# Cosine attention with a feed-forward layer on one core: the order and the size of the first loads

## The chip, the core and the metric

The kernel runs on one core of a Trainium2 chip. The metric is the device time of one launch in microseconds, the median over runs. The profile comes from one further execution, recorded by the hardware profiler.

## What is computed

Batch 8, 12 heads, 448 tokens, head size 64; then a feed-forward layer from 768 to 2048 and back over the 3584 tokens. Inputs and output are float32.

```python
q_n = q / (norm(q, axis=-1) + 1e-6)
k_n = k / (norm(k, axis=-1) + 1e-6)
scores = q_n @ k_n.T / tau                  # tau = 0.1
attn = softmax(scores)                      # over the keys
x = (attn @ v).transpose(0, 2, 1, 3).reshape(B * S, H * D)
h = x @ w_in
out = maximum(0.01 * h, h) @ w_out
```

## The kernel before

**Tiling.** The unit of work on q and k is a pair of heads, a slot `s`; six slots make one batch, and two slots make a quad `j`, for which values are loaded and multiplied together. The 448 tokens of a head are 384 (the main part, 128 partitions with three tokens each) and 64 (the remainder). A pair's tile holds q's three main columns, then a column with q's remainder in partitions 0 to 63 and k's in 64 to 127, then k's three main columns. So q's squares (`squares`, first of the two) read both remainders.

**Steps of a slot.** `squares` squares q and k, on POOL from slot 2 on; for slots 0 and 1 ScalarE and VectorE do it (L523 to L534). `sums` reduces them on VectorE (L195), in two parts. `roots` takes the norms on ScalarE (L202 to L205). `normalise` scales on VectorE (L215, L219) and writes `qn`. `transposes` turns `qn` around on PE (L233) and copies it from PSUM on VectorE (L257); slot 0 has its own copies, half on ScalarE, half on VectorE (L548). `scores` multiplies on PE (L276) and takes exps on ScalarE (L288). `totals` and `products` multiply the exps by ones and by the values on PE (L316), and `scale` writes `xT` on VectorE (L351).

**Order.** The schedule is written out by hand: every engine takes its instructions in the order of the program, and semaphores make it wait for data. The first batch has a prologue of its own, a loop over its six slots (`for s in range(NPAIR)`). In it VectorE takes `sums(n, (1,))` of the slot after next ahead of the qkT copy of the next slot. PE begins with 22 products of constants (`fill(WARM)`, L504). Behind the loop come the third quad's attention, the first feed-forward product of the first block (L374, with `w_in`), and then for each block its second product (L453, L411, with `w_out`) interleaved with the next batch's scores.

**Loads.** q and k come on SP's queue; in the beginning k's first parts are on ScalarE's. `load_first` loads main part (part 0) or remainder (part 1) of `n` slots of the first batch, `load_qk` one slot later on (four DMAs: L144, L145 and twice L147). Values and weights come on POOL's queue and are cast to bf16 on the way: `load_v(j)` a quad's values (L162), `load_v_rem` a batch's remainders (L169), `load_w_in(i)` a quarter of `w_in` (L106; quarters 0 and 1 are the first 1024 columns), `load_w_out` (L113) a half. `hold(x)` is a one-column copy on POOL, which keeps what POOL does next behind the tile `x`.

Of the kernel before, what the change touches and what calls it, by code (L numbers as in the profile page):

```python
# [16 lines left out]
def kernel(  # L17
# [10 lines left out]
    nc = tc.nc  # L28
# [75 lines left out]
    def load_w_in(i):  # L104
        n0, e = i // 2 * (D_ff // 2), i % 2
        gp.dma_start(  # L106
            out=w_in_sb[:, e::2, n0 : n0 + D_ff // 2], in_=w_in_r[e, :, :, n0 : n0 + D_ff // 2]
        )
# [9 lines left out]
    def main(x, b, h0, nh):  # L118
        return x[b, h0 : h0 + nh, 0:MAIN].rearrange("h (p t) d -> p h t d", t=3)
# [4 lines left out]
    def load_first(eng, x, part, s0, n):  # L124

        h0, i = 2 * s0, 0 if x is q else 1
        if part == 0:
            dst = raw0[:, s0 : s0 + n, :, 4 * i : 4 * i + 3]
            eng.dma_start(
                out=dst.rearrange("p s h t d -> p (s h) t d"), in_=main(x, 0, h0, 2 * n)  # L130
            )
        else:
            dst = raw0[64 * i : 64 * i + 64, s0 : s0 + n, :, 3]
            eng.dma_start(
                out=dst.rearrange("p s h d -> p (s h) d"),
                in_=x[0, h0 : h0 + 2 * n, MAIN:S].rearrange("h p d -> p h d"),
            )

    def load_qk(s):
        if s >= NSLOT:  # L140
            return
        b, h0 = s // NPAIR, 2 * (s % NPAIR)
        both = ldp.tile([128, 2, 7, D], F32, name="qk")
        nc.sync.dma_start(out=both[:, :, 0:3], in_=main(q, b, h0, 2))  # L144
        nc.sync.dma_start(out=both[:, :, 4:7], in_=main(k, b, h0, 2))  # L145
        for i, x in enumerate((q, k)):
            nc.sync.dma_start(  # L147
                out=both[64 * i : 64 * i + 64, :, 3],
                in_=x[b, h0 : h0 + 2, MAIN:S].rearrange("h p d -> p h d"),
            )  # L150
        raw[s] = (both[:, :, 0:4], both[:, :, 4:7])
# [5 lines left out]
    def load_v(j):  # L157
        if j >= B * NQ:
            return
        b, jj = divmod(j, NQ)  # L160
        vb[j] = vbp.tile([128, 4, 3, D], BF16, name="v_b")
        gp.dma_start(out=vb[j], in_=main(v, b, 4 * jj, 4))  # L162

    def load_v_rem(b, parts=slice(0, 4)):
        if b >= B:
            return
        x = vrb[b % 2].rearrange("p j g d -> p (j g) d")
        for lo, h0, h1 in ((0, 0, 2), (64, 2, 6), (0, 6, 10), (64, 10, 12))[parts]:
            gp.dma_start(  # L169
                out=x[lo : lo + 64, h0:h1], in_=v[b, h0:h1, MAIN:S].rearrange("h p d -> p h d")  # L170
            )
# [3 lines left out]
    def squares(s, engs=(gp, gp)):  # L175
        if s >= NSLOT:
            return
        tiles = []
        for x, eng, name in zip(raw[s], engs, ("sq0", "sq1")):
            sq = sqp.tile(list(x.shape), F32, name=name)  # L180
            if eng is nc.scalar:
                nc.scalar.activation(sq, x, func=AF.Square)
            else:
                eng.tensor_tensor(sq, x, x, op=ALU.mult)  # L184
            tiles.append(sq)
        sqs[s] = tiles

    def sums(s, parts=(0, 1)):
        if s >= NSLOT:
            return  # L190
        if s not in ss:
            ss[s] = smp.tile([128, 14], F32, name="ss")
        for i in parts:
            o = ss[s][:, 0:8] if i == 0 else ss[s][:, 8:14]
            nc.vector.tensor_reduce(  # L195
                o.rearrange("p (h t) -> p h t", h=2), sqs[s][i], axis=AX.X, op=ALU.add
            )

    def roots(s):
        if s >= NSLOT:  # L200
            return
        nc.scalar.activation(ss[s], ss[s], func=AF.Ln, bias=tiny)  # L202
        nc.scalar.activation(ss[s], ss[s], func=AF.Exp, scale=0.5)  # L203
        if s < 2:
            nc.scalar.activation(ss[s], ss[s], func=AF.Identity, bias=eps)  # L205
# [3 lines left out]
    def normalise(s):  # L209
        if s >= NSLOT:  # L210
            return
        r = smp.tile([128, 14], F32, name="r")
        if s >= 2:
            nc.vector.tensor_scalar_add(ss[s], ss[s], 1e-6)  # L214
        nc.vector.reciprocal(r, ss[s])  # L215
        qn[s] = qnp.tile([128, 7, 2, D], BF16, name="qn")
        for x, lo, hi, r0 in ((raw[s][0], 0, 4, 0), (raw[s][1], 4, 7, 8)):
            nt = hi - lo
            nc.vector.tensor_tensor(  # L219
                qn[s][:, lo:hi],  # L220
                x.rearrange("p h t d -> p t h d"),
                r[:, r0 : r0 + 2 * nt].rearrange("p (h t) -> p t h", h=2)
                .unsqueeze(3).to_broadcast([128, nt, 2, D]),
                op=ALU.mult,
            )
# [35 lines left out]
    def scores(s, kis):  # L261
        key_tiles([(s, ki) for ki in kis])
# [72 lines left out]
    def products(j, e, po=None, begun=False):  # L335
        b, jj = divmod(j, NQ)
        if po is None:
            po = banks(1, (j, e))
        pos[j, e] = po
        vm = vb[j].rearrange("p h t (d e) -> p h t e d", e=2)  # L340
        vr = vrb[b % 2].rearrange("p j g (d e) -> p j g e d", e=2)
        strip_products(
            j, po, lambda g, ki: vm[:, g, ki, e], None if begun else lambda g: vr[:, jj, g, e]
        )
# [123 lines left out]
                store(osb[c, ts], c, chunk_cols(c)[0] + ts * 128, 0, D_model)  # L468
        given_back(("rows", c, two))

    load_first(nc.sync, q, 0, 0, 1)
    load_first(nc.scalar, k, 0, 0, 1)
    load_first(nc.sync, q, 1, 0, 2)
    load_first(nc.scalar, k, 1, 0, 2)
    load_first(nc.sync, q, 0, 1, 1)
    load_first(nc.scalar, k, 0, 1, 1)
    for s, n, r in ((2, 2, 4), (4, 2, 0)):
        for part, m in ((0, n), (1, r)):
            if m:
                for x in (q, k):  # L480
                    load_first(nc.sync, x, part, s, m)
    tiny = cpool.tile([128, 1], F32, name="tiny")
    nc.vector.memset(tiny, 1e-18)
    eps = cpool.tile([128, 1], F32, name="eps")
# [16 lines left out]
    def fill(count):  # L501
        wm = banks(1)
        for i in range(count):
            nc.tensor.matmul(  # L504
                out=wm, lhsT=warm[:, :128], rhs=warm, start=(i == 0), stop=(i == count - 1)
            )
# [4 lines left out]
    def hold(x):  # L511
        seen = smp.tile([128, 1], F32, name="seen")
        gp.tensor_copy(out=seen, in_=x)  # L513
# [21 lines left out]
    normalise(0)  # L535
    load_qk(6)
    hold(qn[0][:, 6, 0, 0:1])
    load_v(0)
    squares(2)
    load_w_in(0)  # L540
    dst = qtp.tile([128, 7, 128], BF16, name="qkT")
    qkT[0] = dst.rearrange("p t c -> p (t c)")
# [11 lines left out]
    for s in range(NPAIR):  # L554
        j = s // 2 - 1 if s >= 2 else None
        even = s % 2 == 0
        n = s + 2 if s + 2 < NPAIR else None
        if s != 3 and s != 5:
            scores(s, (0,))
        if s == 1:  # L560
            roots(2)
        if j is not None and not even:
            products(j, 1)
        scores(s, (1,))
        fill(2)
        if s and n:
            sums(n, (0,))
        if s < 5:
            normalise(s + 1)
            if s != 1 and s < 4:  # L570
                load_qk(s + 7 - (s > 1))
        if j is not None and not even:
            scale(j, 0)
        if s < 5:
            hold(qn[s + 1][:, 6, 0, 0:1])
            squares(s + 3)
        if s == 0:
            load_v_rem(0, slice(2, 4))
        if s < 3:
            load_w_in(s + 1)  # L580
        if s in (1, 3):
            load_v(s // 2 + 1)
        if s == 3:
            load_w_out(0)
        elif s == 4:
            load_w_out(1, 4)
        if n:
            sums(n, (1,))
        scores(s, (2,))
        if s == 5:  # L590

            scale(j, 1)
            for m in range(SOON):
                pms[0, m] = banks(1, (0, m, 0), 4 + m)
            first(0, 0, range(KT - 2))
        elif not even:
            fill(2)
        if not even:
            scores(s, (3,))
        if s < 5:  # L600
            transposes(s + 1)
        if s == 0:
            sums(2, (0,))
        if s == 5:
            first(0, 1, range(KT - 2))
            sums(6)
            sums(7)
        elif not even:
            fill(2)
        if n and s:  # L610
            roots(n)
        if j is not None and not even and s < 5:
            scale(j, 1)
        if j is not None and even:
            totals(j)
            scores(s + 1, (0,))
            products(j, 0)
# [95 lines left out]
    for b in range(B):  # L713
# [15 lines left out]
        s = ready  # L729
# [50 lines left out]
```

## Time and profile before

| | |
|---|---|
| median of 3 runs | 416.69 us (416.69 to 416.94) |
| profiled execution, its own time | 417.32 us |
| its span, first to last instruction | 415.5 us |
| mean granted TensorE clock | 0.996 |
| busy share of PE / ScalarE / VectorE / POOL | 97% / 63% / 47% / 34% |
| HBM read / written | 45.61 MB / 11.01 MB |

The span leaves out what lies around the first and last instruction, here 1.8 us. A PE that counts as busy is not at its peak, since products are pipelined. Idle time of the other engines costs nothing as long as PE does not wait for them. Times within the profile count from the start of the span.

### The profile page before, as it was taken

What the parts mean: (1) busy time and instruction counts of PE and PEld (TensorE: products, weight loads), DVE (VectorE), ACT (ScalarE), POOL (GpSimd) and SP (SyncE); (2) the same over time, 40 slices, a digit from 0 to 9 for tenths busy, and PEclk for the clock granted to TensorE, in tenths of its full rate; (3) what the DMA queues carried; (4) which work ended last, traced back from release to release, by engine and by line L of the source; (5) the groups of instructions that cost most, each with busy time, mean ns of one, the idle gap of its engine ahead of it and who ended that gap; (6) DMA issues with size and microseconds to landing.
All of it is one profiled execution on the core that took longest, in us unless ns stands there. A gap on an engine that the chain in (4) does not pass through costs nothing.

```text
span 415.5 us, 10098 instructions
## 1 busy us (share of the span) xinstructions
PE 402.6 (97%) x4099; PEld 213.6 (51%) x4099; DVE 193.6 (47%) x412; ACT 260.1 (63%) x448; POOL 139.6 (34%) x212
## 2 busy tenths in 40 slices
PE   7687999999999999999999999999999999999996
PEld 2233655544555555544555555544555565544564
DVE  4785856256352725257261645156362654040021
ACT  3785669745785569845775559855776559934300
POOL 2884458055140634054231533153232530000000
PEclk9899999999999999999999999999999999999999
DMA  8999999576485966576386875677387753210023
GB/s 197 248 223 204 213 214 176 160 114 143 97 196 120 124 145 129 128 115 138 92 194 124 114 172 96 134 113 151 91 182 152 106 93 59 65 40 2 0 76 77
DMA packets 104767, 54.21 MB, mean 130 GB/s; under 512 B 70672, under 2 KB 99728, under 8 KB 104720
## 3 DMA queue, kind: packets, MB, share of 16 engines
q1 hardware_dynamic: 78640, 41.21, 42.8%
q0 software_dynamic: 25104, 11.80, 22.7%
q8 instruction: 32, 0.52, 0.6%
q10 hardware_dynamic: 976, 0.56, 0.5%
q14 instruction: 15, 0.12, 0.1%
HBM read 45.61 MB, written 11.01 MB: 136 GB/s over the span
## 4 chain that ended last, share of the span: by engine, by line
PE 91%; DMA 5%; DVE 2%; ACT 1%; POOL 1%; issue 0%; POOLq 0%; ACTq 0%
PE ps L374 35%; PE ps L453 30%; PE ps L316 11%; PE ps L276 7%; PE ps L411 5%; DMA v_b<-in_v_dram 3%; DMA raw<-in_k_dram 1%; PE ps L303 1%; DVE qn L219 1%; POOL sq L184 0%; PE ps L233 0%; DVE ss L195 0%; ACT pe L288 0%; ACT ss L202 0%; POOL w_in_sb L106 0%; DVE r L215 0%
## 5 line engine op out<-in xcount | busy, mean ns | idle before, releaser
L374 PE MATMUL ps<-xT,w_in_sb 128*128 128x384 bf16 (+1 forms) x768 | 147.7, 353 | 0.0
L453 PE MATMUL ps<-w_out_sb,hT 64*128 64x384 bf16 x1536 | 142.7, 323 | 0.0
L288 ACT ACTIVATE pe<-ps 128x896 bf16<-128x896 f32 x144 | 123.3, 918 | 23.2 <-PE ps L276 21.4
L381 ACT ACTIVATE hT<-ps 128x384 bf16<-128x384 f32 (+1 forms) x128 | 67.8, 544 | 73.8 <-PE ps L374 73.0
L374 PEld LDWEIGHTS <-w_in_sb 128*128 128x128 bf16 x768 | 74.2, 98 | 71.3 <-issue 3.4
L453 PEld LDWEIGHTS <-hT 64*128 64x128 bf16 x1536 | 73.6, 94 | 54.9 <-issue 3.3
L184 POOL TENSOR_TENSOR sq<-qk 128x512 f32<-128x512 f32 x84 | 77.4, 942 | 5.9 <-DMA qk<-in_k_dram 3.1
L463 DVE COPY osb<-ps 128x384 f32<-128x384 f32 x48 | 24.5, 553 | 76.0 <-PE ps L453 42.8
L276 PE MATMUL ps<-qkT 64*128 64x448 bf16 (+1 forms) x384 | 54.3, 357 | 3.1 <-ACT pe L288 1.9
L195 DVE TENSOR_REDUCE ss<-sq 128x6 f32<-128x384 f32 (+1 forms) x95 | 54.3, 610 | 0.3 <-POOL sq L184 0.3
L513 POOL CAST seen<-qn 128x1 f32<-128x1 bf16 x48 | 9.0, 187 | 132.9 <-DVE qn L219 125.0
L219 DVE TENSOR_TENSOR qn<-qk,r 128x512 bf16<-128x512 f32 x84 | 50.7, 645 | 1.4
L214 DVE TENSOR_SCALAR ss<-ss 128x14 f32<-128x14 f32 x46 | 9.3, 202 | 68.3 <-ACT ss L203 68.2
L162 POOL DMA_DIRECT2D v_b<-in_v_dram x24 | 18.5, 774 | 65.8 <-PE ps L316 65.8
L351 DVE TENSOR_TENSOR xT<-ps,rb 128x448 bf16<-128x448 f32 x48 | 27.8, 620 | 25.2 <-ACT rb L330 21.8
L316 PE MATMUL ps<-pe,v_b 128*32 128x448 bf16 x576 | 31.9, 353 | 1.8 <-DMA v_b<-in_v_dram 1.8
L276 PEld LDWEIGHTS <-qkT 64*128 64x128 bf16 (+1 forms) x384 | 16.7, 97 | 23.7 <-issue 10.5
L329 ACT ACTIVATE rb<-ps 128x448 f32<-128x448 f32 x24 | 12.9, 539 | 23.8 <-PE ps L316 23.8
L316 PEld LDWEIGHTS <-v_b 128*32 128x32 bf16 x576 | 15.1, 97 | 13.9 <-DMA v_b<-in_v_dram 2.1
L417 DVE COPY osb<-ps 128x384 f32<-128x384 f32 (+1 forms) x9 | 4.6, 514 | 36.6 <-issue 22.6
L288 ACT ACTIVATE pr<-ps 128x896 bf16<-128x896 f32 x24 | 21.3, 921 | 0.3 <-PE ps L276 0.2
L411 PE MATMUL ps<-w_out_sb,hT 128*128 128x384 bf16 (+1 forms) x144 | 21.0, 308 | 0.0
(49 smaller groups left out, 199.2 us busy)
## 6 DMA issues: line engine op xcount, KB each, us to landing
qk<-in_q_dram SPq DMA_DIRECT2D x42, 192.0 KB, 3.2
qk<-in_k_dram SPq DMA_DIRECT2D x42, 192.0 KB, 3.1
out_dram<-osb SPq DMA_DIRECT2D x30, 192.0 KB, 2.8
v_b<-in_v_dram POOLq DMA_DIRECT2D x24, 192.0 KB, 4.4
out_dram<-osb SPq DMA_DIRECT2D x12, 384.0 KB, 2.7
w_in_sb<-in_moe_w_in_dram POOLq DMA_DIRECT2D x4, 768.0 KB, 12.1
w_out_sb<-in_moe_w_out_dram POOLq DMA_DIRECT2D x1, 1536.0 KB, 18.4
w_out_sb<-in_moe_w_out_dram POOLq DMA_DIRECT2D x4, 384.0 KB, 19.7
```

The source lines that it names most:

```text
L184: eng.tensor_tensor(sq, x, x, op=ALU.mult)
L195: nc.vector.tensor_reduce(o.rearrange("p (h t) -> p h t", h=2), sqs[s][i], axis=AX.X, op=ALU.add)
L219: nc.vector.tensor_tensor(qn[s][:, lo:hi], x.rearrange("p h t d -> p t h d"), r[:, r0 : r0 + 2 * nt].rearrange("p (h t) -> p t h", h=2) .u ...
L276: nc.tensor.matmul(out=out[:, a, :S], lhsT=x[rows, c0:c1], rhs=x[rows, 0:S], start=True, stop=True,)
L288: nc.scalar.activation(out=dst, in_=sc[:, :, :S], func=AF.Exp, scale=inv_tau)
L316: nc.tensor.matmul(out=x[32 * g : 32 * g + 32, :S], lhsT=weights(g, ki) if ki < 3 else rem(g), rhs=pe[s][:, ki, a, :] if ki < 3 else pr[j] ...
L351: nc.vector.tensor_tensor(xT[m][:, 2 * jj + e, half * S : (half + 1) * S], pos.pop((j, e))[:, :S], rbs[j], op=ALU.mult,)
L374: nc.tensor.matmul(out=pm[:, :n], lhsT=w_in_sb[:, kt, m * 128 : (m + 1) * 128], rhs=xT[c // 2][:, kt, c0 : c0 + n], start=(kt == 0), stop= ...
L381: nc.scalar.activation(out=hT[c][:, m, :n], in_=pms.pop((c, m))[:, :n], func=AF.Prelu, alpha=0.01)
L411: nc.tensor.matmul(out=po2[:, :n], lhsT=hT[c][:, m, ts * 128 : (ts + 1) * 128], rhs=w_out_sb[:, m, lo : lo + n], start=(m == 0), stop=(m = ...
L453: last[i] = nc.tensor.matmul(out=po2[:, i, :HALF], lhsT=hT[c][rows, m, ts * 128 : (ts + 1) * 128], rhs=w_out_sb[rows, m, half * HALF : (ha ...
L463: nc.vector.tensor_copy(out=osb[c, ts][:, half * HALF : (half + 1) * HALF], in_=po2[:, i, :HALF])
```

## The change

It concerns the loads of the first batch only, and adds or takes away no arithmetic. First, the first batch's loads: pair 0's and pair 1's remainders, fetched by one DMA each for q and k before, are fetched pair by pair, pair 0's on SP's and ScalarE's queues and pair 1's on SP's alone; pair 2 is fetched by itself, then the remainders of pairs 2 and 3, the main part of pair 3, and last pairs 4 and 5 together. SP issues 15 loads ahead of pair 6 instead of 9; ScalarE issues 3 in both. Second, on POOL `squares(2)` stands ahead of `load_v(0)`. Third, the values of quads 1 and 2 are issued one place ahead of the third and of the last quarter of `w_in`; before, they were issued behind the third quarter and one step of the loop behind the last.

```diff
-    load_first(nc.sync, q, 0, 0, 1)
-    load_first(nc.scalar, k, 0, 0, 1)
-    load_first(nc.sync, q, 1, 0, 2)
-    load_first(nc.scalar, k, 1, 0, 2)
+    for part in range(2):
+        load_first(nc.sync, q, part, 0, 1)
+        load_first(nc.scalar, k, part, 0, 1)
     load_first(nc.sync, q, 0, 1, 1)
     load_first(nc.scalar, k, 0, 1, 1)
-    for s, n, r in ((2, 2, 4), (4, 2, 0)):
-        for part, m in ((0, n), (1, r)):
-            if m:
-                for x in (q, k):
-                    load_first(nc.sync, x, part, s, m)
+    for part, s, n in ((1, 1, 1), (0, 2, 1), (1, 2, 2), (0, 3, 1), (0, 4, 2), (1, 4, 2)):
+        for x in (q, k):
+            load_first(nc.sync, x, part, s, n)
...
     normalise(0)
     load_qk(6)
     hold(qn[0][:, 6, 0, 0:1])
+    squares(2)
     load_v(0)
-    squares(2)
     load_w_in(0)
...
         if s == 0:
             load_v_rem(0, slice(2, 4))
+        if s in (1, 2):
+            load_v(s)
         if s < 3:
             load_w_in(s + 1)
-        if s in (1, 3):
-            load_v(s // 2 + 1)
         if s == 3:
             load_w_out(0)
```

## The prediction

> **What bounds the kernel now.** I read the page first: its chain is 91% PE and 5% DMA, and PE is busy for 97% of the span. So the question is where those few per cent lie. The chain in order of time answers it. From 43.01 us on it is PE without a break; ahead of that it runs through loads and VectorE:
>
> ```profile
> 1.30 5.80 DMA raw<-in_k_dram
> 7.19 0.32 ACT sq L526
> ...
> 9.05 1.16 DVE qn L219 x2
> ...
> 12.83 2.41 DVE qn L219 x2
> 15.24 0.46 DVE ss L195
> 15.71 0.61 DVE qkT L257
> ...
> 16.36 0.38 PE ps L276 x2
> ...
> 21.91 0.76 POOL w_in_sb L106
> 22.67 13.26 DMA v_b<-in_v_dram
> ...
> 35.98 1.70 PE ps L316 x32
> ```
>
> Each line is start, duration, what ran. Two loads stand in it, the first remainder of k and the values of the second quad, and one VectorE step (L219) that takes 2.41 us the second time and 1.16 the first. Whatever is gained ahead of 43 us reaches the end whole, because PE does the same work without a break afterwards. Next the timeline, for what each of these steps waits on:
>
> ```profile
> 1.52 7.67 PE L504 MATMUL ps<-warm 128*128 128x512 bf16 x22 [1.52 <-DVE warm L487]
> 9.80 0.81 PE L233 MATMUL ps<-id,qn 128*128 128x128 bf16 x7 [0.61 <-DVE qn L219]
> 12.56 2.27 POOL L184 TENSOR_TENSOR sq<-raw 128x512 f32<-128x512 f32 x2 [1.40 <-DMA raw<-in_q_dram]
> 15.72 1.82 POOL L184 TENSOR_TENSOR sq<-raw 128x512 f32<-128x512 f32 x2
> 35.98 0.75 PE L316 MATMUL ps<-pe,v_b 128*32 128x448 bf16 x12 [1.80 <-DMA v_b<-in_v_dram]
> ```
>
> The bracket is the idle time before the row and what ended it. POOL's squares of pair 2 wait for the remainders of pairs 2 to 5, then run beside the second L219; both are slow (2.27 us against 1.82, 2.41 against 1.16). PE waits 1.80 us for values at 34.18. Last, the table by stretches, for the clock (columns: stretch, busy us of PE, PEld, DVE, ACT, POOL, granted clock, DMA share, GB/s):
>
> ```profile
> 13.93:17.35 3.42, 1.73 (x13) 0.62 (x13) 3.42 (x6) 1.60 (x3) 3.42 (x5) 1.00 1.25 270
> 17.35:20.76 3.41, 3.13 (x17) 1.35 (x17) 2.26 (x7) 3.29 (x7) 3.02 (x6) 0.50 1.09 200
> ```
>
> After a stretch in which PE was half idle, it ran one of 3.41 us at half clock. The DMA share is over 1, so the loads are saturated there: a load put forward is paid for by the ones behind it.
>
> **Pair 0's remainders alone (two heads, 32 KB, not four, 64 KB).** The k remainder was issued at 1.30 and landed at 7.10. Its queue had landed k's main part at 4.31, so 64 KB took 2.79 us more and half of it about 1.4: 5.7 us. Bounds: 4.8 (q's remainder took 0.89 us behind its main part, half of that 0.44) and 7.1. Square, sums, roots and L219 then move up by some 1.4 us, but PE's 22 warm-up products end at 1.52 + 7.67 = 9.19, and the transposes stand behind them. They start at 9.19, not 9.80. The copy behind them on VectorE, the sums of pair 1 behind that copy, and the roots at 11.63 move by those **0.6 us** and no more. For this the remainder need only land by 6.5.
>
> **Pair 1's remainders now go through SP's queue,** fourth and fifth there. ScalarE's squares of pair 1 (L534) wait for them, and behind L534 stands the first qkT copy. Interpolating SP's landings by amount of data (q of pair 1 at 7.36, q of pairs 2 and 3 at 9.15), they land near 7.8; needed by 8.75 if 0.6 us is to be kept. Hidden, by about 1 us.
>
> **Pair 2 by itself.** Before, it is complete when the remainders of pairs 2 to 5 are, 4.87 + 7.6 = 12.4. Now ahead of it lie three pairs instead of four and four remainders instead of six, each remainder counted at half a main part's time (in the trace, packets of 256 B take 18 ns and of 768 B 36 ns). On SP's queue that is the time of 92 main packets per DMA engine, where 72 were done at 9.15 and 104 at 11.0: about 10.2. Bounds: 9.7 (all remainders hidden behind main parts of the other queue), and 16.8 in the slow rival below. POOL's squares then run 10.2 to 12.0. The second L219 begins at 12.83 - 0.6 = 12.23, has no POOL squares beside it, and takes 1.16 as its other cases do: it ends at 13.4, not 15.24. VectorE's sums, the copy, the scores and the exps follow (0.46, 0.61, 0.4): the exps of pair 1 start at 15.0 instead of 16.77. ScalarE is free by 14.4. The front gains **1.8 us**; bounds 0.6 (if L219 still meets the squares) and 2.4 (when ScalarE is free).
>
> **The clock.** PE's idle time between 11.2 and 16.4 shrinks by those 1.8 us, so it is about 66% busy in the stretch that was 51% busy. In the half-rate stretch two warm-ups took 1.04 us against 0.60, the remainder scores 0.59 against 0.38, the transposes 0.93 against 0.55. ScalarE idles only 0.58 us behind this, so at most 0.4 us come back. I take **0.2**, the middle, since only one such stretch is in the trace. The Trainium skill ("TensorE: Matmul & The Clock Gate", Part 1) says that half rate comes after at least one idle stretch of about 3.4 us; here it came after one that was 51% busy, so the trace differs, and by the page's wording the sum would have 0 in this place.
>
> **Values ahead of w_in's third and last quarter.** `load_v(1)` passes one POOL issue (0.78 us); `load_v(2)` passes one `hold`, one pair of squares and w_in's last issue. POOL idles 0.89 us ahead of the hold at 27.20, which covers the extra 0.81 us there. `squares(2)` passes `load_v(0)`, which then issues at 12 instead of 10.4 and lands near 19; first used at 24.94. The transfers go in order: w_in's quarters 2 and 3 land at 30.1 and 34.7, values 1 at 35.94, w_in's last at 39.6, values 2 at 40.68. With the third quarter behind it, values 1 lands at 35.94 - 4.58 = 31.4. PE asks at 34.18 - 2.0 = 32.2, so the **1.8 us** wait goes. Next in line is values 2: without w_in's last quarter (39.63 - 35.94 = 3.7) they land at 37.0. PE uses them at 41.14, so they allow 4.1 us in all, and no stall follows from a gain of 3.8. w_in's last quarter moves to 40.7; its columns start with the ninth block of first products, at about 50 - 4.
>
> **The six extra SP issues.** In the trace, from the fourteenth SP load on, each issue starts when the one eight before it has landed (15.32 behind 15.31, 17.00 behind 16.98). With fifteen loads before pair 6, not nine, pair 6 issues near 10 instead of 8.95 and lands by 18.5; POOL squares it at 27.4 - 2. Hidden, at nothing; uncovered it would cost that 1 us. Later, w_out's last part lands at 60.2, and the loads of pairs 10 to 13 will now start 4 us sooner beside it: it may reach 62, and is used from about 64.
>
> **Sum.** 1.8 + 0.2 + 1.8 = 3.8 us. The profiled execution took 417.32 us (span 415.5), so 413.5; it is 0.6 above the median of 416.69, so by the median **412.9**.
>
> **The rivals.**
> *Values only.* Pair 2 lands at 11.5 or later, L219 still runs beside POOL's squares, and only the transposes' 0.6 us stays of the front: 0.6 + 1.8 = 2.4, giving 414.3. For it: a load issued at 3.21 took 7.8 us, and the ninth SP issue will be near 5.5. Against: that load had 104 such packets ahead, all full.
> *No difference.* PE's wait hangs on the slowest DMA engine, not on the place in the queue: values 1 are nearly all through by 34, two microseconds before they land. If that engine keeps them until 35, and the front keeps nothing, 1 us at most is left: 416.2. Against: w_in ahead of them lands just 1.24 us earlier.
> *Slower: small transfers in series.* VectorE takes the sums of pair 2 ahead of pair 1's qkT copy, so pair 2's last remainder gates pair 1's scores. One SP issue in the trace took 1.88 us. If the fourth to ninth all do, the ninth goes out at 2.6 + 5 x 1.88 = 12.0; with the 4.8 us that a remainder of pair 7 (issued at 13.74) took to land, pair 2 is there at 16.8. Squares, sums, copy and the step to PE add 1.82 + 0.55 + 0.62 + 0.1: scores at 19.9 against 16.36, a loss of 3.5, less the 1.8 of the values: 1.7 slower, 418.4. It takes all the gain from a landing of 15.1 on, and is measurably slower from 16. Against: that 1.88 us issue was a load of twice the size with five large ones unfinished ahead of it.
> The Trainium skill ("DMA: Bandwidth & Descriptors", Rules for kernel authors) speaks for this rival: many small transfers should be joined, and under 64 KB mostly overhead is paid. Its fixed cost of about 2 us for each of the two more transfers ahead of pair 2, if paid in series, would put pair 2 at 14.2, and by that the kernel would gain about 1 us. Here 192 KB landed 3.2 us after issue and 64 KB 3.6, so a fixed part is there, but four transfers were under way at once.
>
> **How the numbers follow.** Forecast 0.66; values only 0.17; no difference 0.06; slower 0.11. A measurement can tell 0.2%, some 0.8 us, from no change. Faster is forecast and values only, 0.83; same 0.06; slower 0.11. The range reaches down to 411.8 (the front at 2.4, the clock at 0.4, values 1.8 and the 0.25 us by which runs of before differ, with values 2 some 0.7 us earlier than worked out) and up to 415.0 (values only, with half of the wait for values left); outside lie about 0.2.
>
> **What would show it.** Right: the row with in_k's remainder ends before 6.5; the seven transposes (L233) start at 9.2 straight behind the warm-ups; POOL's first squares start near 10.2 without the 1.40 us wait behind a load; the second L219 takes under 1.5 us for its two; no half clock near 17 to 21; the first `v_b` products have no wait for DMA, start near 32.2, and PE goes unbroken from about 39.2. Wrong: L534 or POOL's first squares waiting for a remainder past 11; PE waiting for `v_b` at either place; a wait for `w_in_sb` or `w_out_sb` behind 43 us, where there is none now.

## The result and the profile after

The kernel after takes 415.03 us, median of five runs (414.21 to 415.49); five runs of before on the same chip gave 416.69. The ratio is 0.9955, 95% interval 0.994 to 0.997: 1.66 us faster, less than half of the 3.8 us forecast. The profiled execution took 415.49 us, span 413.7, clock 0.996; against the 415.5 of before the span is 1.8 shorter.

First the end of the chain (start, duration, what ran), to be laid beside the chain of before. From 40.89 us on it is PE, and what PE waits for last are again values, now those of quad 2:

```profile
23.30 15.85 DMA v_b<-in_v_dram
39.19 1.70 PE ps L316 x28
40.89 3.68 PE ps L374 x22
```

Further back the chain runs through a load of pair 6, but that link is no wait. It hangs VectorE's L219 at 20.08 on a load that landed at 20.29, when L219 had begun; the timeline has L219 0.04 us behind the reciprocal of L215. Who ended a wait is inferred, so a link like this one is worth a look at the rows beside it. What did change is in SP's own timeline (start and duration of an issue):

```profile
4.62 0.47 SPq L129 DMA_DIRECT2D raw<-in_k_dram  x1
6.77 0.61 SPq L134 DMA_DIRECT2D raw<-in_q_dram  x1
```

The seventh load of SP went out at 4.62, the eighth at 6.77, straight behind the landing of q of pair 1, which was issued at 2.04 and landed at 6.75. SP's waits in the first 30 us name the same (us in total, times, longest):

```profile
SPq L134 <- DMA raw<-in_q_dram: 1.7, 1, 1.7
```

What the DMA engines did meanwhile, in the table by stretches (stretch, busy us of PE, PEld, DVE, ACT, POOL, granted clock, DMA share, GB/s). Before:

```profile
6.00:8.00 2.00, 2.00 (x8) 0.79 (x7) 0.29 (x1) 0.46 (x2) 0.00 (x0) 1.00 1.05 347
8.00:10.00 2.00, 1.39 (x10) 0.54 (x8) 1.19 (x3) 1.61 (x5) 1.60 (x3) 1.00 1.25 238
```

After:

```profile
6.00:8.00 2.00, 2.00 (x10) 0.71 (x8) 1.00 (x3) 1.75 (x5) 0.92 (x2) 1.00 0.74 210
8.00:10.00 2.00, 1.82 (x15) 0.72 (x14) 1.94 (x5) 0.69 (x3) 0.85 (x3) 1.00 0.56 90
```

The share falls from over 1 to 0.74 and 0.56, and the rate from 238 to 90 GB/s. By 11 us the DMA records of before add up to 2185 KB, those of after to 1750: 435 KB had not been fetched (a KB is 1024 bytes here). They are not made up later: by 31 us it is 6768 KB against 6288. The front itself came early, as the timeline of after shows (start, us, engine, line, operation, count; in brackets the idle time before and what ended it):

```profile
8.14 0.81 PE L233 MATMUL ps<-id,qn 128*128 128x128 bf16 x7
10.18 1.82 POOL L184 TENSOR_TENSOR sq<-raw 128x512 f32<-128x512 f32 x2 [1.32 <-DMA raw<-in_k_dram]
11.18 1.84 DVE L219 TENSOR_TENSOR qn<-raw,r 128x512 bf16<-128x512 f32 x2
14.54 0.92 ACT L288 ACTIVATE pe<-ps 128x896 bf16<-128x896 f32 x1 [1.26 <-PE ps L276]
...
32.59 0.75 PE L316 MATMUL ps<-pe,v_b 128*32 128x448 bf16 x12 [1.38 <-DMA v_b<-in_v_dram]
39.19 0.75 PE L316 MATMUL ps<-pe,v_b 128*32 128x448 bf16 x12 [1.07 <-DMA v_b<-in_v_dram]
73.76 0.55 PE L276 MATMUL ps<-qkT 64*128 64x448 bf16 x4 [0.46 <-DMA qkT<-qn]
```

The exps of pair 1 start at 14.54, against 16.77 before: 2.2 us. But PE waits for values twice, 1.38 + 1.07 us, where it waited 1.80 once, and at 73.76 there is a wait that before did not have. The first feed-forward products behind the third quad (L374) begin at 40.82 (before 42.95): 2.1 us there, 1.5 us behind the wait of 0.46 (the values' remainders, L303, at 77.57 against 79.07), 1.8 at the end of the span.

### The profile page after: what moved, and what is told of

The parts are those of the page before. It is cut to its first block, busy times and chain, and to the rows that moved or that the text cites. A ratio compares the mean times of both kernels' runs of the same rounds, so it can differ in the third digit from the quotient of the medians.

```text
span 413.7 us, 10099 instructions
## 1 busy us (share of the span) xinstructions
PE 400.9 (97%) x4088; PEld 213.6 (52%) x4099; DVE 193.2 (47%) x412; ACT 259.9 (63%) x448; POOL 139.4 (34%) x212
## 4 chain that ended last, share of the span: by engine, by line
PE 88%; DMA 8%; SPq 2%; POOL 0%; DVE 0%; issue 0%; POOLq 0%
PE ps L374 35%; PE ps L453 29%; PE ps L316 10%; PE ps L276 7%; PE ps L411 5%; DMA v_b<-in_v_dram 4%; DMA qk<-in_q_dram 2%; DMA qkT<-qn 1%; PE ps L303 1%; DMA raw<-in_q_dram 1%; SPq L134 1%; SPq L129 1%; POOL sq L184 0%; PE ps L233 0%; DVE qn L219 0%
## 5 line engine op out<-in xcount | busy, mean ns | idle before, releaser
L374 PE MATMUL ps<-xT,w_in_sb 128*128 128x384 bf16 (+1 forms) x760 | 147.3, 352 | 0.4
L374 PEld LDWEIGHTS <-w_in_sb 128*128 128x128 bf16 x768 | 74.1, 98 | 71.3 <-issue 3.4
L219 DVE TENSOR_TENSOR qn<-qk,r 128x512 bf16<-128x512 f32 x84 | 51.4, 653 | 2.0 <-DVE r L215 0.6
L214 DVE TENSOR_SCALAR ss<-ss 128x14 f32<-128x14 f32 x46 | 8.8, 190 | 67.6 <-ACT ss L203 67.6
```

The lines of the kernel that those rows point to most:

```text
L219: nc.vector.tensor_tensor(qn[s][:, lo:hi], x.rearrange("p h t d -> p t h d"), r[:, r0 : r0 + 2 * nt].rearrange("p (h t) -> p t h", h=2) .u ...
L374: nc.tensor.matmul(out=pm[:, :n], lhsT=w_in_sb[:, kt, m * 128 : (m + 1) * 128], rhs=xT[c // 2][:, kt, c0 : c0 + n], start=(kt == 0), stop= ...
```

## Experiments

**The theory, T.** The gain of the front is real, and it is spent on the values because the DMA engines run dry between 6 and 10 us. They run dry because SP stands until an earlier load has landed, while few bytes are under way and the next loads are small. The letters of the rivals are those of the expectations. The first four kernels were timed beside before at 416.64 us, the next four at 416.61.

**Values alone** (before, with only their order changed):

```diff
+        if s in (1, 2):
+            load_v(s)
         if s < 3:
             load_w_in(s + 1)
-        if s in (1, 3):
-            load_v(s // 2 + 1)
```

> The kernel before with the third part of the change alone: values of quads 1 and 2 one place ahead of w_in's third and last quarter; first loads and squares(2) as before. Theory T (the change saves PE's wait for values, but its small first loads leave the DMA idle: SP and ScalarE share eight completion semaphores, and SP stood from 5.09 to 6.77 us for the landing of q of pair 1; 435 KB fewer were moved by 11 us, some 2.1 us of DMA time, and that is missing when the values land): here the first loads are the old ones, so values 1 land near 31.4 and values 2 near 37.0, PE waits for neither, and the gain is the 1.8 us of the old wait: 414.9 us. Rival R1 (the place in POOL's queue counts for less than worked out, the slowest DMA engine sets the landing): values 2 land near 39, as in the changed kernel, and values 1 near 32.5; then the time is also about 414.9, but the landings tell the two apart.

Measured: 414.76 us, ratio 0.994 (0.9919 to 0.9962). The values of quads 1 and 2 land at 31.73 and 36.54, and in the timeline neither product has a bracket:

```profile
33.07 0.75 PE L316 MATMUL ps<-pe,v_b 128*32 128x448 bf16 x12
38.42 0.74 PE L316 MATMUL ps<-pe,v_b 128*32 128x448 bf16 x12
```

The third part of the change, by itself, gains 1.9 us: the 1.8 that the prediction gave it. It is as fast as the whole change.

**Loads alone** (after, with the values in their old places: the same edit taken back).

> The changed kernel with the values back in their old places (behind w_in's third quarter, and one step of the loop behind its last). Theory T: the front is some 2.2 to 2.9 us early as in the changed kernel, but the DMA is 2.1 us behind, so values 1 land near 38 instead of 35.9, PE waits about 6 to 7 us for them, and the kernel is slower than before by about 2 us: 418.7 us. Rival R1 (the small loads cost the DMA nothing, the places of the values were mis-sized): values 1 land at 35.9 as before and the time is that of before, 416.7 us, within 0.3.

Measured: 419.49 us, ratio 1.0055 (1.0036 to 1.0073): slower than before by 2.9 us. Only 1734 KB had come by 11 us. The values of quad 1 land at 36.06, where T said 38 and R1 35.9, so on this landing T was wrong and R1 right. They were issued earlier, though, at 21.40 against 22.67 in before, and took 14.66 us against 13.26. The loss showed in another way. PE came early and waited longer, and ran the next stretch at half clock, as timeline and table by stretches have it:

```profile
36.11 0.75 PE L316 MATMUL ps<-pe,v_b 128*32 128x448 bf16 x12 [3.19 <-DMA v_b<-in_v_dram]
36.96 1.35 PE L316 MATMUL ps<-pe,v_b 128*32 128x448 bf16 x12
```

```profile
33.37:36.78 3.41, 0.67 (x16) 0.43 (x20) 0.00 (x0) 1.27 (x2) 3.15 (x5) 1.00 1.22 230
36.78:40.20 3.42, 3.42 (x30) 0.87 (x22) 2.10 (x4) 0.92 (x1) 0.00 (x0) 0.50 1.25 203
```

PE was busy for 0.67 us of 3.41, then twelve products took 1.35 us and not 0.75. This execution took 418.66 us; ten runs lie between 417.16 and 420.10. The values of quad 2 land at 42.22, the values' remainders (L303) are multiplied at 80.74 (before 79.07).

**The same eighteen loads in another order** (after; pair 1's remainders go out ahead of q of pair 1, so the load whose landing SP waits for is a small and early one):

```diff
+    for x in (q, k):
+        load_first(nc.sync, x, 1, 1, 1)
     load_first(nc.sync, q, 0, 1, 1)
     load_first(nc.scalar, k, 0, 1, 1)
-    for part, s, n in ((1, 1, 1), (0, 2, 1), (1, 2, 2), (0, 3, 1), (0, 4, 2), (1, 4, 2)):
+    for part, s, n in ((0, 2, 1), (1, 2, 2), (0, 3, 1), (0, 4, 2), (1, 4, 2)):
```

> The changed kernel with the same 18 transfers of the same sizes on the same queues, but pair 1's two remainders are issued on SP ahead of q's main part of pair 1. By the rotation of the eight semaphores the loads from the seventh SP issue on then wait for small transfers that land at about 5, not for q of pair 1 (6.755 in the changed kernel). Theory T with the wait as its cause: SP's stand from 5.09 to 6.77 is gone, by 11 us 250 to 350 KB more have been moved than the changed kernel's 1750, values 2 land near 37.5 to 38, and the time is 413.3 to 414.0 us. Rival R2 (not the wait, but the 0.5 to 0.65 us that SP takes for each small issue starves the DMA): SP issues earlier, but bytes at 11 us rise by under 100 KB and the time stays at 414.7 to 415.0.

Measured: 413.01 us, ratio 0.9897 (0.9871 to 0.9923), an interval apart from that of after. In the timeline SP's eighth load (the first row) goes out at 5.30, not 6.77, behind the landing of pair 1's q remainder at 5.29, and the values are there when PE asks:

```profile
5.30 0.61 SPq L134 DMA_DIRECT2D raw<-in_q_dram  x1
...
31.55 0.75 PE L316 MATMUL ps<-pe,v_b 128*32 128x448 bf16 x12
36.98 0.75 PE L316 MATMUL ps<-pe,v_b 128*32 128x448 bf16 x12
```

And by stretches the DMA engines stay busy from 8 us on:

```profile
8.00:10.00 2.00, 1.84 (x15) 0.76 (x16) 1.89 (x5) 0.66 (x2) 0.18 (x1) 1.00 1.04 222
```

By 11 us 2175 KB had come, 425 more than after. The front is no faster than that of after (exps of pair 1 at 14.62), so the 2.0 us come from what is behind it: values 1 at 31.02 and 2 at 36.94 (after 32.55 and 39.15), and the products of L374 that follow begin at 38.61 (40.82). Neither the number nor the size of the transfers has changed, so these did not cost it, and R2 falls.

**Remainders of pairs 1 to 3 on POOL's queue** (after; SP is rid of four small loads):

```diff
-            load_first(nc.sync, x, part, s, n)
+            load_first(gp if part and s < 4 else nc.sync, x, part, s, n)
```

> The changed kernel with the four remainder loads of pairs 1, 2 and 3 issued from POOL, whose completion semaphores are its own, and which idles until 7 us; SP has 11 loads ahead of pair 6 instead of 15. Theory T: fewer loads pass through the eight semaphores and SP gets to the large ones sooner; bytes by 11 us come back to near the 2185 KB of before (over 2000), values 2 land near 37.2, PE's two waits for values are under 0.3 us in all, and the time is 412.8 to 413.5 us, unless remainders of pair 1 land later than 8 from this queue. Rival R2 expects nearly the same, since SP also issues fewer small loads; rival R1 (landings set by the slowest engine) expects 414.5 to 415.0, with values 2 still near 39.

Measured: 412.74 us, ratio 0.9893 (0.9872 to 0.9914). By stretches and in the timeline:

```profile
8.00:10.00 2.00, 1.92 (x16) 0.72 (x14) 2.00 (x5) 1.26 (x3) 2.00 (x5) 1.00 1.07 288
```

```profile
11.29 1.16 DVE L219 TENSOR_TENSOR qn<-raw,r 128x512 bf16<-128x512 f32 x2
13.97 0.92 ACT L288 ACTIVATE pe<-ps 128x896 bf16<-128x896 f32 x1 [0.58 <-PE ps L276]
...
70.72 0.55 PE L276 MATMUL ps<-qkT 64*128 64x448 bf16 x4 [0.50 <-DMA qkT<-qn]
```

The share is over 1, 2377 KB had come by 11 us, values 1 and 2 land at 29.29 and 36.07, and the products of L374 begin at 37.74. This is what the prediction had drawn for the change itself, with L219 at 1.16 us. SP stands here too: its seventh load goes out at 7.28, 2.0 us behind the end of the sixth issue, and this costs nothing. The wait of half a microsecond for pair 11's `qkT` is left.

**Six tiny loads** (values alone, plus six SP loads of 256 B each into a tile that nothing reads, at three places among the first loads; the large loads stay large):

```diff
+    def tiny_loads(i):
+        for n in (i, i + 1):
+            nc.sync.dma_start(out=scrap[:, n], in_=q[0, 0, n : n + 1])
```

> The kernel of the first experiment (old first loads, new order of the values) with six more SP loads of 256 bytes into a tile that nobody reads: two each behind q of pair 1, behind the main parts of pairs 2 and 3, and behind the remainders of pairs 2 to 5. So SP has 15 loads ahead of pair 6, as in the changed kernel, but every real load keeps its old size and order. Theory T (a load holds one of eight semaphores and half a microsecond of SP's time however small it is): fewer bytes are under way, SP stands for the landing of earlier loads, 200 to 450 KB less than the first experiment's 2238 are moved by 11 us, values 2 land 1 to 2.5 us later than its 36.5, and the time rises from 414.8 to 415.5 to 417. Rival R3 (what costs is the size of the split loads themselves, the overhead of small transfers within the DMA engines): 1.5 KB more do nothing, bytes at 11 us within 100 KB of 2238, time within 0.5 of 414.8.

Measured: 414.06 us, ratio 0.9932 (0.9917 to 0.9947). T expected a loss and there was none: it is no slower than values alone. SP did stand, as the timeline shows (these two tiny loads take 1.48 us with what is between them), and 227 KB less had come by 11 us:

```profile
5.32 1.48 SPq L475 DMA_DIRECT2D scrap<-in_q_dram  x2
```

But by stretches the engines were not dry behind it:

```profile
8.00:10.00 2.00, 1.40 (x11) 0.60 (x10) 2.00 (x5) 1.12 (x3) 1.30 (x3) 1.00 1.12 267
```

While SP stood, the main parts of pairs 2 and 3, two large transfers, were under way. The values land at 31.74 and 36.54, as without the tiny loads. So T has to be narrowed: more loads and a standing SP are not enough; few bytes must also be in flight. The traces of the five kernels let that be added up. At 8.0 us the loads of q, k and values that had been issued, less the bytes that had been moved, came to about 850 KB in before, 70 in after, 460 in the reordered kernel, 745 with the remainders on POOL and 490 here. By 31 us the last three had moved 6674, 6770 and 6652 KB, near the 6768 of before; after was at 6288.

**A later place for pairs 13 and 14** (the kernel with the remainders on POOL; their loads go one step later, behind the transposing DMAs of pairs 10 and 11, whose place in SP's queue is the disputed matter, theory D):

```diff
-        load_qk(s + 4)
+        for n in {9: (), 10: (13,), 11: (14, 15)}.get(s, (s + 4,)):
+            load_qk(n)
```

> The kernel with the remainders on POOL, and on SP's queue the loads of pair 13 and pair 14 each one step later, behind the transposes by DMA of pair 10 and pair 11. In that kernel, as in the changed one, PE waits 0.5 us at 70.7 for pair 11's transposed tile, which was issued at 64.6 and landed at 70.7, behind loads of pairs 13 and 14; before, it was issued at 69.1 and landed in 3.5 us. Theory D (the backlog of the DMA, met some 4 us sooner, now makes the transposes late): without those loads in front the tile lands by 69, the wait is gone, and the time is 412.2 to 412.4. Rival: the tile is late because of w_out and the values on POOL's queue, which share the DMA engines; then the wait stays and the time is 412.7.

Measured: 412.6 us, ratio 0.9897 (0.9883 to 0.9912). Pair 11's transposing DMA lands 3.7 us after its issue, and the products of 70.98 have no bracket:

```profile
65.77 1.26 SPq L251 DMA_TRANSPOSE qkT<-qn  x1
...
70.98 0.54 PE L276 MATMUL ps<-qkT 64*128 64x448 bf16 x4
```

The late wait is therefore one behind loads in the same queue. Its worth is not settled by the time. The same kernel without this edit was run again beside it:

> The kernel with the remainders of pairs 1 to 3 on POOL once more, beside the next two on the same chip: 412.7 us as before.

It gave 413.59 us, ratio 0.9914 (0.9895 to 0.9933), where it had given 412.74; the intervals of all three overlap, so between 0.1 and 1.0 us is all that can be said. Nor do the profiles settle it: in that of the later place PE waits 0.6 us for the values of quad 2, which it does not in the first profile of the kernel without the edit. The two profiles of one and the same kernel differ in the clock: one has no stretch at half rate behind 6 us, the other has one at 14.55.

**Values back in their old places, with the remainders on POOL:**

> The kernel with the remainders on POOL, with the values back in their old places. Theory T: with the DMA no longer starved the front is about 2.4 us early, PE asks for values 1 near 30.5, and they land where 4.6 us of w_in's third quarter put them, near 34; PE waits some 3.5 us, at most 1.5 to 2 us are gained, and if the wait is followed by a stretch at half clock as in the second experiment, nothing: 414.8 to 416.7 us. Rival R1 (the place of the values counts for little): 412.7 to 413.2.

Measured: 417.14 us, ratio 1.002 (0.9999 to 1.0041), somewhat above T's band and far from R1's. In the timeline PE waits for values twice:

```profile
34.51 0.75 PE L316 MATMUL ps<-pe,v_b 128*32 128x448 bf16 x12 [1.83 <-DMA v_b<-in_v_dram]
40.59 0.75 PE L316 MATMUL ps<-pe,v_b 128*32 128x448 bf16 x12 [0.56 <-DMA v_b<-in_v_dram]
```

Even with the DMA engines fed, an earlier front brings nothing without the values' new order. All of it together, each as the recorded ratio to before, which differs by up to 0.16% from the quotient of the medians:

| first loads | values in old places | values ahead of w_in |
|---|---|---|
| as before | 1 | 0.9940 |
| as in the change | 1.0055 | 0.9955 |
| the same loads, pair 1's remainders first | not run | 0.9897 |
| remainders of pairs 1 to 3 on POOL's queue | 1.0020 | 0.9893, again 0.9914 |

The last two rows of the right column beat both kernels, by 3.0 to 3.9 us against before; so does the kernel with pairs 13 and 14 put back, 4.0 us.

## Why the prediction was only partly right

**Where it held.** The direction and most landings did. The k remainder of pair 0 landed at 5.34 (worked out: 5.7), pair 1's last remainder at 7.35 (7.8), pair 2 was complete at 10.0 (10.2), POOL's first squares ran at 10.18, and PE's transposes followed straight behind the warm-ups, at 8.14 instead of 9.2, because the full clock was granted earlier in this execution (from 4.78 us, not 7.11). The earlier clock is luck, and so in part is the landing of pair 2. It was worked out from a queue in which packets follow each other without a gap, but its remainders were issued at 6.77 and 7.43, behind SP's stand, and the last of them landed at 10.0 from engines whose share was 0.56. The order of the values was worth what was said, shown by itself. The rule that under 64 KB mostly overhead is paid (the Trainium skill, "DMA: Bandwidth & Descriptors", Rules for kernel authors), which had spoken for the slower rival, does not decide here: the eighteen transfers of after and of its reordered twin are the same, and the twin is 2.0 us faster.

**The failed step** is "The six extra SP issues ... Hidden, at nothing". The prediction had seen that an issue waits for the landing of the load eight before it, but counted SP's loads alone, "from the fourteenth SP load on", and looked for the price at pair 6 (which went out at 11.63, not near 10). The trace of before showed it sooner: SP's sixth load went out at 3.99, behind the landing of its first at 3.97, and its seventh at 4.87, behind its second at 4.86. The issue records name the semaphores: the loads of SP and ScalarE take eight in turn (101, 102 and 104 to 109). In after SP's third load signals 104, and its eighth, the next to use 104, waits for it. With ScalarE's three counted in, that is eight loads apart in this turn, and in the reordered kernel the eighth issue again follows SP's third landing (5.30 behind 5.29). For 1.7 us SP could issue nothing, and what came next were two loads of 64 KB at 0.65 us an issue.

**What hung on it** is the sentence "The transfers go in order", with values 2 "at 37.0". It took the DMA engines to be saturated throughout, as they were before. With 435 KB less by 11 us, SP's later loads (pairs 8 and 9) were still running beside the values: pair 9 landed at 37 to 39.3, before at 30 to 35. The traffic of SP's queue between 29 and 38 us was 615 KB, before 100, in the reordered kernel 296. Values 1 came at 32.55 (worked out: 31.4), values 2 at 39.15. So in place of a term of +1.8 for the values' wait stand 1.80 us of waiting before against 2.45 after, a loss of 0.65, and 0.46 for `qkT` later.

**Terms that were off in size.** The front gained 2.2 us, not 1.8; some 0.5 of that differs between executions whose front is the same (16.77 in before, 16.23 with the values alone changed). POOL's first squares still waited 1.32 us for a load. The second L219 did not take 1.16: it began at 11.18, still met 0.8 us of POOL's squares and took 1.84; it takes 1.16 where pair 2's squares are out of its way. The 0.2 for the clock was 0: the half-rate stretch came back, 15.02 to 18.43, behind a stretch in which PE was 1.83 of 3.42 us busy. A gain that the sum did not have is a wait of PE for pair 5's `qn`, which after does not have (timeline, before and then after):

```profile
32.20 0.81 PE L233 MATMUL ps<-id,qn 128*128 128x128 bf16 x7 [0.63 <-DVE qn L219]
```

```profile
29.30 0.76 PE L233 MATMUL ps<-id,qn 128*128 128x128 bf16 x7
```

All three kernels with the values in their old places have it (0.62 or 0.63 us), none of the others does, so it belongs to the order of the values. In these three VectorE's L214 ahead of it takes 0.91 or 0.92 us, not 0.16 to 0.20, and ends within 0.01 us of POOL's issue of a load of `w_out`, beside which it runs; why, no run here tests. The sum by the measured terms is 2.2 + 0.63 - 0.65 = 2.2 us up to the last values, behind which PE's products (L374) begin 2.1 earlier. The 0.3 us that the end of the span regained is not traced to single steps.

**Of the rivals,** *values only* named a time (414.3) not far off, and L219 did run beside POOL's squares, but the rest of its reason is contradicted by the runs: pair 2 landed at 10.0, not at 11.5 or later, and the front gained more than 0.6 us. *Small transfers in series* had a standing SP right and its place wrong: the price was not on pair 2 but on what was issued behind it.

## What to carry to other kernels

Before a large first load is split, list all loads in order of issue across the queues that share their completions, mark the one whose landing each issue must wait for, and see that enough bytes are in flight at that moment; a small, early load in that place costs nothing, and a late one empties the DMA engines where little else is in flight. A load put forward is only worth what the next load lets through: here an earlier front lost up to 2.9 us without the values' order and gained 1 to 2 us on top of it once the engines stayed fed. Check the DMA share stretch by stretch ahead of a sum that assumes transfers "go in order".

## What was unexpected of the hardware

Half-rate stretches of the clock last 3.41 us or twice that, and their phase differs from execution to execution. In eight of the ten profiles the first one behind the warm-up begins between 14.55 and 17.35 us, each time 10.24 us, three stretches of 3.41, behind the start of full clock; two profiles of one kernel have one and none. In these eight the stretch just ahead had PE busy for 1.0 to 1.8 us, so PE was not idle; in the two profiles without one, for 2.1 and 2.4. By stretches (PE busy is the first figure behind the comma), the kernel with the remainders on POOL, second run:

```profile
11.14:14.55 3.41, 1.59 (x14) 0.69 (x13) 2.96 (x6) 2.80 (x6) 3.41 (x7) 1.00 1.20 255
14.55:17.96 3.41, 3.41 (x17) 0.92 (x16) 2.74 (x7) 3.21 (x6) 3.07 (x7) 0.50 1.18 180
```

The Trainium skill ("TensorE: Matmul & The Clock Gate", Part 1) says that the window is free-running and does not start with the kernel. The different phases agree with that; the busy 1.59, 1.73 and 1.83 us ahead of half rate differ from its one idle window. The busy time of one stretch does not settle it, either: before has a later stretch with 1.85 us busy (34.41 to 37.83), and the kernel with the remainders on POOL and the values in their old places one with 1.58 (32.07 to 35.48), and neither has half rate behind it. What else counts stays open.

A transposing DMA within the chip's memory shares the fate of the loads ahead of it in SP's queue: pair 11's landed 3.7 us after its issue with two pairs' loads moved behind it, and held PE up by 0.5 us with them in front.
